# A planned attention and expert kernel: the first three pairs' operands prepared another way, EPS moved into the sums' tiles, and the order planned again

## The chip, the cores and the metric

The kernel runs on one core of one Trainium2 chip. The metric is device microseconds of one execution. The engines are called PE (TensorE, matmul), DVE (VectorE), ACT (ScalarE), POOL (GpSimd) and SP (SyncE, which here issues most of the transfers; POOL issues the rest).

## What is computed

Windowed attention with a linear position bias over 8 batches of 8 heads (S = 576, D = 64), whose output x (8 x 576 x 512) goes into a layer of four attention experts, of which each position takes the two that its gate ranks highest:

```python
scores = scale * q @ k.T                       # per batch and head, 576 x 576
scores = where((rel >= 0) & (rel < 128), scores + slope[h] * -abs(rel), -1e9)
attn = exp(scores - max);  attn /= attn.sum(-1) + 1e-9
x = (attn @ v) with the heads side by side     # B, 576, 512
w = softmax over the top 2 of x @ w_gate       # of 4 experts
for e in range(4):
    a = exp(causal(scale * (x @ wq[e]) @ (x @ wk[e]).T) - max);  a /= a.sum(-1) + 1e-9
    out += w[e] * (a @ (x @ wv[e]) @ wo[e])
```

All of it is float32, and the matmuls run on pairs of rounded operands: a high part and the low rest.

## The kernel before

The heads are taken two at a time: 32 pairs, g = 0 to 31, four to a batch. A pair's raw q and k come in as one tile `r` (128 partitions: one head's 64 dimensions on the upper half and the other's on the lower; q in columns 0 to 575, k in the rest). From it the kernel wants `h`, which holds the rounded high part of q and of k in a layout of its own, the low rest of q written into the other half of the same tile (`h<-r,h` in the rows), and the low rest of k in `klA` (`klA<-r,h`). Two subtractions on half of the partitions each make the one, and two the other; they run on DVE for the pairs 0 and 3 and on POOL else.

Before the change the high part of pair 0 comes by two transfers that POOL issues (`in_hd` holds the same numbers already laid out, and the transfer rounds them), that of pair 1 is rounded on the chip by eight copies from `r` (`rnd`, L428: on POOL or ACT), and from pair 2 on it comes by one POOL transfer a pair (`load_hi`, L499). There are two `h` buffers and one raw buffer `r`; pair 1's `r` lies in a buffer of the tag `v2`, which the expert part uses later (`load`, L480).

Then a pair goes through: scores `s` on PE from h and klA; mask (`COPY_PREDICATED` with `mkt`) and bias with the row's minimum into `nm` on DVE, `p` by an exponential on ACT (`p<-p,nm`) that also leaves the row's sum in `sm`; `normalise` (L606) on DVE adds EPS to the sums (`r<-sm`) and takes the reciprocal, and nine scalings of p by it (`p<-p,r`, `scl`, L434: POOL or ACT, each 128x128) follow; transposes `t` on PE, `pa` on DVE or ACT, the output `x` on PE, and its high and low part `xh` on ACT and DVE. When a batch's four pairs are through, the expert part projects `xh` with the weights WH and WL (made at the start from four staged loads `wst`), and again makes scores `ms`, exponentials `mp`, sums `msm`, `moe_norm` (L856: `mr<-msm`, then scalings on POOL), transposes, values and the output rows `ot`. KHm, QSm, QZm, AHm, AHTm are high parts of its operands, rounded copies that may lie on more than one engine. The attention of the next batch runs beside the experts of the last.

The order is not the order in the text. Every operation is recorded, those that `nc.any` names with several engines, and `plan` (L364) builds the dependence graph and runs a list scheduler (`schedule`, L248) over it: each operation has a rank by its distance to the end plus an offset by the kind of tile it writes (`K['off']`, one number for a kind and an engine), an operation with a choice goes to the engine on which it would be done first by the planner's costs (`_cost`, L57), weighted and biased by `wt`, `bv`, `ba` and `bp`, and a result that crosses engines is charged a latency that `K['lm']` lengthens. Where PE has nothing to do before a set time, the planner puts in a filler, a 128x256 matmul on the zeroed tile QZm that is never read (`warm`, L542; its name in the rows is `warm<-QZm`). All engines then run the planned order, fixed at build time. Since every operation is issued from one place, all rows of the trace name line L1130.

```python
rnd(qs[0][d, :S], r[dn, :S])      # load_hi, d = up, dn: 64x576, two of the eight roundings of pair 1
rnd(kh[0][d], r[up, S:])
```

Of the kernel before, what the change touches and what calls it, by code (L numbers as in the profile page):

```python
# [10 lines left out]
F32 = mybir.dt.float32  # L11
F32R = mybir.dt.float32r
# [22 lines left out]
K = {'sub': '01101', 'S': 2, 'T': 2, 'A': 2, 'X': 1, 'M': 1, 'apv': 0, 'alag': 2, 'pvlag': 2, 'vorder': 0, 'na': 0, 'pp': 2, 'tp': 4, 'mp': 4, 'ta0': 0.08, 'ta1': 0.91, 'sa0': 0.1, 'sa1': 1.0, 'sb0': 0.68, 'sb1': 0.77, 'tb0': -0.03, 'tb1': 1.08, 'wo0': 0.1, 'wo1': 0.45, 'wa0': 0.05, 'wa1': 1.3, 'aa0': 0.0, 'aa1': 1.04, 'ab0': -0.04, 'ab1': 1.0, 'xp': 5, 'sp': 'h||q0 k0|q1|k1', 'ts': 1, 'lead': 0, 'pa': 1, 'na0': 2, 'wb0': 0.18, 'wb1': 1.0, 'sh': 0, 'man': 1, 'mode': 'rank', 'wv': 1, 'off': {'AHms': -17666, 'QSmv': -252, 'outs': -101984, 'KHmg': -413974, 'mps': -362123, 'mrv': -147, 'mptls': -12718, 'hv': 201556, 'mst': 544, 'klv': -1407, 'mpv': -164993, 'wsts': -39692, 'idts': 30423, 'mslt': -3598, 'pv': 145397, 'ots': -67973, 'wv': 612, 'QSms': 238851, 'malt': 978, 'mpts': 16944, 'mtlt': 925, 'pg': -121184, 'mat': -557, 'QDmg': 12259, 'QDmv': 8479, 'AHTms': 59664, 'rv': 59092, 'xtt': 172643, 'vv': 20187, 'vts': -31342, 'rs': 41611, 'cntv': 129924, 'mtt': 1799, 'MPLv': -1030, 'ALTmv': -3669, 'exv': -3931, 'WLv': -330, 'pas': -78677, 'mtts': -135375, 'klg': -78, 'MPLg': -2850, 'tbts': -14292, 'mpg': 26252, 'QZmv': -10712, 'ps': 33824, 'tmts': -456520, 'tms': -205980, 'ALmv': -22397, 'WOHg': -11820, 'WOLv': 42451, 'vs': 5270, 'Qv': 221304, 'KLmg': 67871, 'exs': -162797, 'vg': 16350, 'wsv': 1100, 'wg': -45799, 'MPLs': -10841, 'klAv': 118649, 'xhs': 143747, 'vt': 847, 'mkts': -1800, 'exg': 12657, 'Gg': -11111, 'mxv': -5689, 'KLmv': -28553, 'sv': 8239, 'xhv': 131107, 'klAg': 17772, 'WHg': -29134, 'hg': 26552, 'pav': 144, 'ot': -5058, 'qkt': -18, 'KHms': -16548, 'tt': 859, 'st': 2712}, 'cw': 6, 'lm': 85, 'f0': 900, 'f1': 69640, 'f2': 6176, 'e0': 0, 'setup': 7620, 'wt': 1.0164, 'bv': 4000, 'ba': 634, 'bp': 3635, 'chn': 150, 'e1': 1, 'wu': 0, 'r1': 1, 'l0': 0.5, 'l1': 0.75, 'w0': 0.04, 'w1': 0.83, 'w2': 0.15, 'w3': 1.15}  # L35
# [21 lines left out]
def _cost(e, m, a, k):  # L57
# [20 lines left out]
    return (260 if isinstance(a[2], float) else 244) + 0.84 * n  # L78


def _half(a):
    if a[0].ap[0][1] != D:
        return 0
    return 1 if a[0].offset // a[0].ap[0][0] < D else 2
# [74 lines left out]
def graph(ops, alt):  # L159
# [49 lines left out]
    return dict(port=port, half=half, cat=cat, nodes=nodes, two=two, pred=pred, eng=eng, cost=cost, alts=alts, cols=cols, dma=dma, kind=kind, lab=lab)  # L209
# [38 lines left out]
def schedule(g, rank, succ, setup=0.0, wt=0.5, bias=(0, 0, 0, 0, 0), fill=(900, 60000, 9999), cw=6):  # L248
# [22 lines left out]
    while done < n:  # L271
        while ev and ev[0][0] <= now:
            i = heapq.heappop(ev)[1]
            q = alts[i]
            if len(q) > 1:
                r = rank[i]
                best = None
                for x, (e, c) in enumerate(q):
                    f = max(t[e], now) + c + wt * c + bias[e]
                    for z, j in ready[e]:  # L280
                        if -z > r:
                            f += cost[j]
                    if best is None or f < best[0]:
                        best = (f, e, c, x)
# [5 lines left out]
        for e in range(5):  # L290
            if not ready[e] or t[e] > now:
                continue
            if e == 0 and setup and len(ready[0]) > 1:
# [4 lines left out]
                i = best[1]  # L298
            else:
# [11 lines left out]
            elif e < 4:  # L311
                if half[i] and last[e] and half[i] != last[e]:
                    s = max(s, t[e] + 125)
# [904 lines left out]
```

## Time and profile before

| | us |
|---|---|
| median of 3 runs | 604.6 (603.01 to 606.43) |
| the profiled execution, its own time | 604.72 |
| its span, first to last instruction | 603.0 |
| PE busy | 579.4 (96%), 4697 matmuls |
| ACT busy | 509.5 (84%) |
| DVE busy | 425.9 (71%) |
| POOL busy | 301.1 (50%) |

Busy time counts instructions that overlap once. In rows of a group, the busy time divided by the count is what one instruction takes of its engine; the mean in ns that stands beside it contains the overlap with the next. The granted clock of PE is given as a share of 2.4 GHz: 1.00 is that level and 0.50 is 1.2 GHz.

### The profile page before, as it was taken

Reading aid. Unit: us, or ns where it says so; the run is one execution under the profiler, and the core shown is the slowest. Engines: PE = TensorE matmul, PEld = TensorE weight load, DVE = VectorE, ACT = ScalarE, POOL = GpSimd, SP = SyncE. Lnnn points to the kernel's source line nnn. Section 1 sums busy time; section 2 is a strip of 40 time slices with the busy share of each in tenths; the row PEclk is TensorE's granted clock in tenths of the full one; section 3 lists DMA queues with packets and bytes.
Section 4 is the critical chain, followed back from the end, with each engine's and each line's share of the span. In section 5 each row is a group of like instructions: output and inputs, shape, how many; then the busy total and the mean of one; then the engine's idle time right before and its main releaser. Section 6 shows DMA issues by size and latency. Waiting matters only on the chain.

```text
span 603.0 us, 14062 instructions
## 1 busy us (share of the span) xinstructions
PE 579.4 (96%) x4697; PEld 493.6 (82%) x4697; DVE 425.9 (71%) x1768; ACT 509.5 (84%) x1745; POOL 301.1 (50%) x366
## 2 busy tenths in 40 slices
PE   7999999999999999999999999999999999999996
PEld 7978898788878897888878897888987888789764
DVE  3699869867886689666985689756896669544730
ACT  1987979998989889988999988898999888775973
POOL 3826645676466445473656445674455632023430
PEclk8999999999999999999999999999999999999999
DMA  8496745423544444524345335434444400110013
GB/s 310 133 322 209 248 134 196 146 68 118 168 133 165 146 146 145 198 76 143 107 169 190 123 108 175 154 108 146 143 147 178 155 27 23 54 36 2 1 53 106
DMA packets 24857, 81.50 MB, mean 135 GB/s; under 512 B 2385, under 2 KB 3153, under 8 KB 24785
## 3 DMA queue, kind: packets, MB, share of 16 engines
q1 hardware_dynamic: 16336, 42.00, 21.1%
q0 software_dynamic: 8448, 38.60, 19.0%
q8 instruction: 37, 0.61, 0.4%
q14 instruction: 36, 0.29, 0.2%
HBM read 71.16 MB, written 9.44 MB: 134 GB/s over the span
## 4 chain that ended last, share of the span: by engine, by line
PE 47%; ACT 27%; DVE 15%; DMA 4%; issue 4%; POOL 2%; ACTq 0%; POOLq 0%; DVEq 0%
ACT p L1130 11%; PE qk L1130 8%; PE v L1130 8%; PE s L1130 5%; PE o L1130 5%; PE mt L1130 5%; PE ms L1130 4%; DVE pa L1130 3%; PE t L1130 3%; ACT KHm L1130 3%; ACT mp L1130 3%; PE ma L1130 3%; PE x L1130 2%; DVE r L1130 2%; DVE p L1130 2%
## 5 line engine op out<-in xcount | busy, mean ns | idle before, releaser
L1130 ACT ACTIVATE p<-p,nm 128x128 f32<-128x128 f32 x288 | 113.2, 396 | 29.2 <-DVE nm L1130 28.2
L1130 POOL TENSOR_TENSOR h<-r,h 64x576 fp32r<-64x576 f32 x60 | 85.2, 1420 | 90.5 <-DMA h<-in_hd 55.7
L1130 PE MATMUL qk<-xh,WH 128*128 128x288 f32 x512 | 115.8, 306 | 1.1 <-ACT xh L1130 0.8
L1130 POOL TENSOR_SCALAR mp<-mp,mr,w 128x128 f32<-128x128 f32 (+3 forms) x128 | 76.0, 606 | 64.9 <-DVE mr L1130 57.5
L1130 ACT ACTIVATE p<-p,r 128x128 f32<-128x128 f32 x288 | 98.7, 398 | 9.7 <-DVE r L1130 8.4
L1130 PE MATMUL s<-h 128*128 128x256 f32 (+2 forms) x320 | 87.0, 296 | 3.1 <-DVE h L1130 1.8
L1130 PEld LDWEIGHTS qk<-xh,WH 128*128 128x128 f32 x512 | 84.4, 189 | 4.2 <-ACT xh L1130 1.1
L1130 POOL TENSOR_TENSOR klA<-r,h 64x576 fp32r<-64x576 f32 x60 | 85.2, 1420 | 2.4
L1130 PE MATMUL s<-klA,h 128*128 128x256 f32 (+2 forms) x320 | 84.1, 281 | 0.2 <-POOL klA L1130 0.2
L1130 DVE TENSOR_TENSOR pa<-t,tmt 128x512 f32<-128x512 f32 (+2 forms) x96 | 73.9, 772 | 10.0 <-PE t L1130 6.1
L1130 DVE CUSTOM_DVE_ANT_0 p<-s,tbt 128x128 f32<-128x128 f32 x288 | 72.4, 286 | 3.3 <-PE t L1130 0.6
L1130 ACT ACTIVATE mp<-mp,mnm 128x256 f32<-128x256 f32 (+3 forms) x128 | 71.5, 562 | 3.8 <-DVE mnm L1130 3.5
L1130 DVE COPY_PREDICATED s<-mkt,s 128x256 f32<-128x256 int32 (+2 forms) x160 | 52.6, 331 | 29.9 <-PE s L1130 28.9
L1130 PEld LDWEIGHTS s<-h 128*128 128x128 f32 x320 | 60.5, 190 | 15.3 <-issue 7.2
L1130 PE MATMUL qk<-xh,WL 128*128 128x288 f32 x256 | 71.0, 302 | 0.0
L1130 DVE CUSTOM_DVE_ANT_0 mp<-ms,mtt 128x128 f32<-128x128 f32 (+3 forms) x128 | 59.7, 486 | 15.1 <-PE ms L1130 13.5
L1130 PE MATMUL v<-WH,xh 128*128 128x260 f32 x288 | 65.8, 297 | 0.2 <-DVE lg L1130 0.2
L1130 PE MATMUL x<-pa,vt 128*64 128x256 f32 (+1 forms) x512 | 62.7, 359 | 0.5 <-DVE pa L1130 0.5
L1130 PEld LDWEIGHTS s<-klA,h 128*128 128x128 f32 x320 | 60.6, 192 | 1.2 <-issue 0.6
L1130 PE MATMUL mt<-idt,mp 128*128 128x128 f32 x320 | 59.3, 277 | 1.8 <-DVE ALTm L1130 0.4
L1130 PE MATMUL t<-idt,p 128*128 128x128 f32 x288 | 52.5, 277 | 7.2 <-ACT AHm L1130 2.0
L1130 ACT ACTIVATION_READ_ACCUMULATOR p<-p,nm 128x1 f32 x288 | 54.8, 190 | 0.0
(112 smaller groups left out, 1389.5 us busy)
## 6 DMA issues: line engine op xcount, KB each, us to landing
h<-in_hd POOLq DMA_DIRECT2D x30, 1216.0 KB, 6.4
r<-in_rd SPq DMA_DIRECT2D x31, 576.0 KB, 3.9
vt<-in_vd SPq DMA_DIRECT2D x32, 320.0 KB, 3.1
out<-ot SPq DMA_DIRECT2D x32, 256.0 KB, 2.0
wst<-in_wall SPq DMA_DIRECT2D x4, 386.0 KB, 4.8
h<-in_hd POOLq DMA_DIRECT2D x2, 608.0 KB, 7.7
out<-ot SPq DMA_DIRECT2D x8, 128.0 KB, 2.3
r<-in_rd SPq DMA_DIRECT2D x2, 288.0 KB, 3.0
```

What stands on the lines that cost most here:

```text
L1130: getattr(getattr(tc.nc, e), m)(*a, **k)
```

## The change

**The beginning.** Pair 0's high part is now rounded on the chip, by eight copies that may also go to DVE (`rnd3`), and pair 1's comes by a POOL transfer. Pair 2's goes by two POOL transfers into two of the four expert buffers `mp` that are not yet in use, and pair 2's raw tile into a third. The raw tile of pair 1 and its values come ahead of most tables on SP's queue, the output weights and later tables behind pair 2's raw tile.

**EPS.** The sums get a place of their own with EPS as a neighbouring element, set once at the start (`SM`, `MSM`). A reduction over each sum and its neighbour takes the place of the addition of a constant: 64 `r<-sm` and 48 `mr<-msm` on DVE. Eight small copies `lg<-lg` become additions from PSUM.

**The planner.** Its rule for engines that switch between upper and lower partitions looks at the output and the first input, operations on ACT, DVE and POOL are chosen so that such switches are fewer (`hs`), offsets and biases are given apart for four phases of the program (the beginning, batch 0, the middle, the last batch), `lm` falls from 85 to 15, and all offsets are new. As built, 106 of the 288 scalings `p<-p,r` move from ACT to POOL (3 to 5 of the nine of a pair, from pair 5 on), with them 23 of 64 second roundings of KHm (`KHm<-KHm`) and 14 of 32 `QZm<-QSm`; 9 of 16 `AHTm`, 5 of 16 `AHm` and 4 of 32 `xh<-xt` move from ACT to DVE. There are 181 fillers in place of 209.

```diff
-K = {'sub': '01101', ... 'off': {...}, 'lm': 85, ... 'setup': 7620, 'wt': 1.0164, 'bv': 4000, 'ba': 634, 'bp': 3635, ...}
+K = {'wd': 0, 'sub': '01101', ... 'off': {...}, 'lm': 15, ... 'setup': 8000, 'wt': 0.6887, 'bv': 322, 'ba': -520, 'bp': -651, ...
+     'hs': 5017, 'h4': 'cdmd', 'ra': 'rvm', 'bz': [10885, -12379, 30216]}
 def _half(a):
-    if a[0].ap[0][1] != D:
-        return 0
-    return 1 if a[0].offset // a[0].ap[0][0] < D else 2
+    x = [q for q in a[:2] if _is_ap(q)]
+    return sum((q.offset // q.ap[0][0] >= D) << i for i, q in enumerate(x))
 def schedule(...):
+            elif 0 < e < 4 and hs and len(ready[e]) > 1:
+                best = min(heapq.nsmallest(cw, ready[e]), key=lambda q: q[0] + (hs if half[q[1]] != last[e] else 0))
...
+    def rnd3(dst, src):
+        nc.any(
+            ("gpsimd", "tensor_scalar", (dst, src, 1.0, 0.0), dict(op0=mul, op1=add)),
+            ("scalar", "copy", (dst, src), None),
+            ("vector", "tensor_copy", (dst, src), None),
+        )
+    SM = [cp.tile([P, 9, 2], F32, name=f"sm{k}") for k in range(2)]
+    MSM = [cp.tile([P, 19], F32, name=f"msm{k}") for k in range(2)]
 def load(g):
+        home = K["ra"][g] if g < len(K["ra"]) else "r"
-        if g == 1 and K["r1"]:
+        if home == "v":
             r = m1.tile([P, NQ + 1, E * D], F32, tag="v2", ...)
+        elif home == "m":
+            r = m1.tile([P, 10 * P], F32, tag="mp", name=f"r{g}", bufs=K["mp"])[:, : 2 * S]
 def load_hi(g):
+        how = K["h4"][g] if g < len(K["h4"]) else "d"
+        if how == "m":
+            hh = [m1.tile([P, 10 * P], F32R, tag="mp", name=f"h{g}_{k}", bufs=K["mp"])[:, :o1] for k in range(2)]
...
-        if (g or K["e0"]) and g <= K["e1"]:
+        if how == "c":
             for d in (up, dn):
-                rnd(qs[0][d, :S], r[dn, :S])
-                rnd(kh[0][d], r[up, S:])
+                rnd3(qs[0][d, :S], r[dn, :S])
+                rnd3(kh[0][d], r[up, S:])
...
+        elif how == "m":
+            for k in range(2):
+                o = (o1 + P) * k
+                nc.gpsimd.dma_start(hh[k], hd[b, p, :, o : o + o1])
 def normalise(g, c0, c1):
-        nc.vector.tensor_scalar(r[:, c0:c1], sm[:, c0:c1], EPS, None, op0=add)
-        nc.vector.reciprocal(r[:, c0:c1], r[:, c0:c1])
+        nc.vector.tensor_reduce(r, sm[:, c0:c1, :], AX.X, add)
+        nc.vector.reciprocal(r, r)
 def moe_norm(b, pr, j):
-            nc.vector.tensor_scalar(r, sm[:, 4 * j : 4 * j + 4], EPS, None, op0=add)
+            nc.vector.tensor_reduce(r, sm[:, 8 * j : 8 * j + 8].rearrange("p (a n) -> p a n", n=2), AX.X, add)
 def zero():
+            nc.vector.memset(SM[k][:, :, 1], EPS)
+            nc.vector.memset(MSM[k][:, 1:16:2], EPS)
+            nc.vector.memset(MSM[k][:, 18:19], EPS)
 # the beginning of the program
+    load(1)
+    nc.sync.dma_start(loaded_vt[0], vd[0, 0])
     load_const_b()
     prep0()
-    load(1)
```

Three places of the planned order show it. First PE at the start, before the change; `warm2` is the filler, s0_0 to s0_4 are the five score tiles of pair 0:

```order
L1130 MATMUL warm2_112<-QZm_99 128x256 x26
L1130 MATMUL s0_0_118<-h0_110 128x128
L1130 MATMUL warm2_112<-QZm_99 128x256 x3
L1130 MATMUL s0_1_120<-h0_110 128x256
L1130 MATMUL warm2_112<-QZm_99 128x256 x6
L1130 MATMUL s0_0_118<-klA0_96,h0_110 128x128
```

and now:

```order
L1163 MATMUL warm2_116<-QZm_103 128x256 x37
L1163 MATMUL s0_0_121<-h0_114 128x128
L1163 MATMUL s0_0_121<-klA0_100,h0_114 128x128
L1163 MATMUL s0_0_121<-h0_114 128x256
L1163 MATMUL s0_0_121<-klA0_100,h0_114 128x256
L1163 MATMUL s0_1_123<-h0_114 128x256
```

The first block of fillers has grown from 26 to 37, and the scores of pair 0 follow in one piece.

Second, ACT at the start, before the change; h1 and r1 belong to pair 1, p0 and p1 to the pairs 0 and 1, WOH is the high part of the output weights:

```order
L1130 ACT_TABLE_LOAD
L1130 ACTIVATE p0_117,sm0_116<-p0_117,nm0_115 128x128 x4
L1130 CAST WOH_94<-wst4_162 128x1024
L1130 ACTIVATE p0_117,sm0_116<-p0_117,nm0_115 128x128 x3
L1130 CAST h1_119<-r1_113 64x576 x2
L1130 ACTIVATE p0_117,sm0_116<-p0_117,nm0_115 128x128 x2
L1130 CAST h1_119<-r1_113 64x576 x5
L1130 ACTIVATE p0_117<-p0_117,r0_0_122 128x128
```

and now:

```order
L1163 ACT_TABLE_LOAD
L1163 CAST h0_114<-r0_112 64x576 x8
L1163 ACTIVATE p0_120,sm0_96<-p0_120,nm0_119 128x128 x6
L1163 ACTIVATE p0_120<-p0_120,r0_0_125 128x128 x5
L1163 ACTIVATE p0_120,sm0_96<-p0_120,nm0_119 128x128 x3
L1163 ACTIVATE p0_120<-p0_120,r0_5_128 128x128 x4
```

The seven roundings of pair 1 are gone from between the exponentials of pair 0, and eight roundings of pair 0 stand ahead of them.

Third, POOL some pairs in, before the change; h6, h7 and klA belong to the pairs 6 and 7:

```order
L1130 TENSOR_TENSOR h6_217<-r6_211,h6_217 64x576 x2
L1130 TENSOR_TENSOR klA0_96<-r6_211,h6_217 64x576 x2
L1130 TENSOR_TENSOR h7_239<-r7_233,h7_239 64x576 x2
L1130 TENSOR_TENSOR klA1_97<-r7_233,h7_239 64x576
L1130 DMA h8_261<-in_hd 128x2x1216
L1130 TENSOR_TENSOR klA1_97<-r7_233,h7_239 64x576
```

and now:

```order
L1163 TENSOR_TENSOR h6_216<-r6_211,h6_216 64x576 x2
L1163 DMA h7_237<-in_hd 128x2x1216
L1163 TENSOR_TENSOR klA0_100<-r6_211,h6_216 64x576 x2
L1163 TENSOR_SCALAR p5_214<-p5_214,r5_5_229 128x128 x2
L1163 TENSOR_SCALAR KHm_106<-KHm_106 64x288
L1163 TENSOR_TENSOR h7_237<-r7_232,h7_237 64x576 x2
L1163 TENSOR_TENSOR klA1_101<-r7_232,h7_237 64x576
L1163 DMA h8_258<-in_hd 128x2x1216
L1163 TENSOR_TENSOR klA1_101<-r7_232,h7_237 64x576
L1163 TENSOR_SCALAR p6_235<-p6_235,r6_5_250 128x128 x2
```

Scalings of p (of pairs 5 and 6) and a rounding of KHm now stand in POOL's queue behind the subtractions that need a transferred h, and ahead of the next ones.

## Rows read from the trace of the kernel before

**Rows 1.** The page, part 1 (busy time, share of the span and instructions of each engine) and part 4 (the chain that ended last, by engine).
```profile
PE 579.4 (96%) x4697; PEld 493.6 (82%) x4697; DVE 425.9 (71%) x1768; ACT 509.5 (84%) x1745; POOL 301.1 (50%) x366
...
PE 47%; ACT 27%; DVE 15%; DMA 4%; issue 4%; POOL 2%; ACTq 0%; POOLq 0%; DVEq 0%
```

**Rows 2.** Busy time in four stretches: the stretch and its length, then PE, PE's weight loads, DVE, ACT and POOL with their instructions, the granted clock, the DMA share and GB/s.
```profile
0.00:75.00 75.00, 70.19 (x547) 61.45 (x548) 55.75 (x208) 54.91 (x198) 41.35 (x44) 0.98 0.73 244
75.00:525.00 450.00, 437.48 (x3622) 374.21 (x3621) 338.35 (x1430) 400.64 (x1403) 238.56 (x285) 1.00 0.40 133
525.00:560.00 35.00, 34.93 (x264) 30.10 (x262) 17.30 (x74) 25.07 (x72) 9.18 (x19) 1.00 0.08 24
580.00:604.00 24.00, 17.51 (x129) 12.51 (x127) 2.45 (x8) 10.33 (x23) 2.27 (x4) 0.94 0.28 100
```

**Rows 3.** The timeline of PE at the start (start, duration, engine, line, operation, tiles, and the idle time before with what ended it), and the fillers as a whole (count, duration min/median/max in ns, first and last start).
```profile
1.53 5.88 PE L1130 MATMUL warm<-QZm 128*128 128x256 f32 x26 [1.53 <-DVE QZm L1130]
9.19 0.33 PE L1130 MATMUL s<-h 128*128 128x128 f32 x1 [1.78 <-DVE h L1130]
...
16.71 4.36 PE L1130 MATMUL warm<-QZm 128*128 128x256 f32 x35
...
L1130 PE MATMUL warm<-QZm x209: 274/283/581, 1.5 to 68.7; 128*128 128x256 f32 x105
```

**Rows 4.** Two stretches at the start, columns as in group 2.
```profile
7.40:9.20 1.80, 0.02 (x2) 0.01 (x1) 0.48 (x2) 0.00 (x0) 0.00 (x0) 1.00 1.04 355
10.60:14.00 3.40, 3.40 (x19) 3.40 (x18) 2.87 (x11) 0.41 (x3) 0.00 (x0) 0.51 1.04 403
```

**Rows 5.** Transfers, the page's part 6: count, KB each, median us from issue to landing.
```profile
h<-in_hd POOLq DMA_DIRECT2D x30, 1216.0 KB, 6.4
...
h<-in_hd POOLq DMA_DIRECT2D x2, 608.0 KB, 7.7
...
r<-in_rd SPq DMA_DIRECT2D x2, 288.0 KB, 3.0
```

**Rows 6.** The timeline of ACT at the start, and one row of POOL's, columns as in group 3.
```profile
13.59 0.40 ACT L1130 ACTIVATE p<-p,nm 128x128 f32<-128x128 f32 x1 [11.58 <-DVE nm L1130]
...
17.37 1.37 ACT L1130 CAST h<-r 64x576 fp32r<-64x576 f32 x2
...
19.55 3.44 ACT L1130 CAST h<-r 64x576 fp32r<-64x576 f32 x5
...
23.61 0.39 ACT L1130 ACTIVATE p<-p,nm 128x128 f32<-128x128 f32 x1
...
0.73 1.05 POOL L1130 MEMSET KLm<- 64x1152 f32 x1 [0.29 <-POOLq L1203]
```

**Rows 7.** Groups of instructions on ACT: count, busy us, mean ns of one, idle time before them and what ended it.
```profile
L1130 ACT ACTIVATE p<-p,r 128x128 f32<-128x128 f32 x288 | 98.7, 398 | 9.7 <-DVE r L1130 8.4 <-DVE lg L1130 0.5
L1130 ACT CAST KHm<-KHm 64x288 fp32r<-64x288 f32 x64 | 26.9, 430 | 1.0
L1130 ACT CAST AHm<-ma 128x512 fp32r<-128x512 f32 x16 | 9.2, 576 | 0.6 <-PE ma L1130 0.5
L1130 ACT CAST QZm<-QSm 128x64 fp32r<-128x64 f32 x32 | 7.5, 242 | 1.2 <-DVE QSm L1130 0.5
L1130 ACT CAST h<-r 64x576 fp32r<-64x576 f32 x7 | 4.7, 672 | 0.2
```

**Rows 8.** Groups of instructions on POOL, columns as in group 7.
```profile
L1130 POOL TENSOR_TENSOR h<-r,h 64x576 fp32r<-64x576 f32 x60 | 85.2, 1420 | 90.5 <-DMA h<-in_hd 55.7 <-issue 15.2 <-DMA r<-in_rd 15.2
...
L1130 POOL DMA_DIRECT2D h<-in_hd x32 | 24.1, 753 | 39.2 <-PE s L1130 26.2 <-PE v L1130 10.4 <-PE t L1130 1.5
...
L1130 POOL TENSOR_SCALAR mp<-mp,mr,w 128x128 f32<-128x128 f32 x32 | 14.3, 446 | 64.8 <-DVE mr L1130 57.5 <-ACT AHm L1130 3.4 <-ACT KHm L1130 1.2
```

**Rows 9.** Waits of ACT and of POOL between 75 and 525 us: who waited for whom, us in total, times, longest.
```profile
ACT p L1130 <- DVE nm L1130: 14.5, 26, 1.3
...
POOL h L1130 <- DMA h<-in_hd: 55.7, 9, 7.9
```

**Rows 10.** The timeline of POOL at 18 and 28 us and of DVE at 30 and 40 us, columns as in group 3.
```profile
18.03 0.66 POOL L1130 TENSOR_SCALAR h<-r 64x576 fp32r<-64x576 f32 x1
...
28.68 2.93 POOL L1130 TENSOR_TENSOR klA<-r,h 64x576 fp32r<-64x576 f32 x2
...
30.34 1.31 DVE L1130 TENSOR_SCALAR r<-sm 128x4 f32<-128x4 f32 x1
...
40.55 0.17 DVE L1130 TENSOR_SCALAR r<-sm 128x4 f32<-128x4 f32 x1
```

**Rows 11.** Groups of instructions on DVE, columns as in group 7.
```profile
L1130 DVE TENSOR_SCALAR r<-sm 128x5 f32<-128x5 f32 x32 | 13.0, 406 | 3.9 <-ACT p L1130 3.8
L1130 DVE TENSOR_SCALAR r<-sm 128x4 f32<-128x4 f32 x32 | 10.2, 320 | 6.8 <-ACT p L1130 6.5
L1130 DVE TENSOR_SCALAR mr<-msm 128x4 f32<-128x4 f32 x32 | 9.0, 282 | 14.8 <-ACT mp L1130 13.0 <-ACT AHTm L1130 1.6 <-POOL mp L1130 0.2
L1130 DVE TENSOR_SCALAR mr<-msm 128x1 f32<-128x1 f32 x16 | 3.4, 210 | 4.4 <-ACT MPL L1130 4.3
L1130 DVE TENSOR_REDUCE ws<-ex 128x5 f32<-128x20 f32 x8 | 1.4, 171 | 0.8 <-POOL ex L1130 0.7
```

**Rows 12.** ACT alone from its first exponential to 75 us: length, busy time and instructions, then clock, DMA share and GB/s.
```profile
13.59:75.00 61.41, 53.63 (x197) 1.00 0.69 231
```

## What is predicted

> **What bounds the kernel now.** I read the page's shares first: PE is busy for 96% of the span and ACT for 84%, and of the chain that ended last 47% is PE and 27% ACT [rows 1]. So PE bounds it, and what can be won is idle time of PE, PE work that does nothing, and PE work at the lower clock. Next I cut the span into stretches [rows 2]. In the steady part, 75 to 525 us, PE is idle for 450.0 - 437.5 = 12.5 us (2.8%) with ACT busy for 400.6 of 450 (89%). From 525 to 560 us, where the last batch's attention is over, ACT is at 25.1 of 35 (72%) and PE idle for 0.07 us (0.2%). That pair of rows makes ACT a suspect for PE's gaps, not more: DVE and POOL have less to do there too.
>
> The third view is the timeline of PE at the start [rows 3]. Most of it is filler: 26 of them from 1.53 us, then nothing to 9.19 us, where the first score of pair 0 starts, and 35 between 16.71 and 21.1 us, where PE has done pair 0's scores and waits for pair 1's. The fillers count as busy, so the 94% of the first 75 us [rows 2] is not work. The fourth view is the granted clock in small stretches [rows 4]: 1.00 from 7.40 to 9.20 us, 0.51 from 10.6 to 14.0. The lower level is 1.2 GHz; what lies ahead of it is that 1.8 us, in which PE ran almost nothing (0.02 us). The end, 580 to 604 us [rows 2], has the same output rows behind it in both orders, and I expect nothing there.
>
> **The beginning.** Before, pair 0 waits for its h, which two transfers on POOL's queue bring 7.7 us after their issue, while its raw tile lands after 3.0 us [rows 5]. ACT does nothing of weight until its first exponential at 13.59 us [rows 6]. Now eight roundings from the raw tile make h on ACT in that free time. The raw tile is the first transfer on SP's queue, issued when the engines start at 0.7 us [rows 6], so they start at about 0.7 + 3.0 = 3.7 us; one takes 4.7 / 7 = 0.67 us of ACT [rows 7], the first seven end at about 3.7 + 7 x 0.67 = 8.4 us, and the fillers planned ahead last to 7.41 + 11 x 4.36 / 35 = 8.8 us [rows 3]. So the roundings are covered by fillers, and the cover is 0.4 us; if the raw tile lands later than that, PE stands still again. Three terms follow:
> - 28 fillers fewer (209 to 181) at 4.36 / 35 = 0.125 us [rows 3]: -3.4 us. A filler is only padding, so this is real only as far as the waits it covered are shorter too; the next paragraph checks that on ACT.
> - The hole of 1.8 us between 7.40 and 9.20 [rows 4] is closed: -1.8 us.
> - Without the hole I expect no fall of the clock: 3.4 us ran at half the clock [rows 4], and the same work at 2.4 GHz takes half: -1.7 us.
>
> Together -6.9 us. The check by ACT: the first exponential can come at about 10.1 us instead of 13.59, because the seventh rounding ends at 8.4 and the scores, the mask and the bias need the rest (-3.5), and the seven roundings of pair 1 that stood among pair 0's exponentials, 1.37 + 3.44 us [rows 6], leave ACT's queue (-4.7). So ACT allows at most 8.2 us. The lower bound is 0: the time could be lost again at the next wait. What is late next is pair 1. Its h now comes by one transfer of 1216 KB; issued at about 3.1 us, behind two POOL memsets of 1.05 us that begin at 0.73 [rows 6] and two small ones, it lands at 9.5 us by the median of 6.4 [rows 5], up to 1.3 later by the 7.7 us that the first two took while the tables loaded. Behind it four POOL subtractions of 1.42 us and 0.75 us of the issue of pair 3's transfer [rows 8] end at 16 to 17.3 us. By then ACT has nine exponentials and nine scalings of pair 0 to do from 10.1 us on, which end near 17 us. So the new wait is about covered, and I take the 6.9, which lies near the upper bound because three rows carry it one by one.
>
> **The steady part.** What leaves ACT, each by busy time over count [rows 7]: 106 scalings of p at 0.343 (36.3 us), 23 KHm at 0.420 (9.7), 14 QZm at 0.234 (3.3), 5 AHm at 0.576 (2.9), and 9 AHTm and 4 xh of the same 128x64 as the QZm at up to 0.234 (3.0): 55.2 us, of which I put nine tenths, some 49 us, into 75 to 525 us. ACT falls to (400.6 - 49) / 450 = 78%. On a straight line between 89% (PE idle 2.8%) and 72% (0.2%) that is 1.1%, a gain of 7.5 us. Since the quiet stretch is quiet on other engines too, I take half of PE's idle time, -6.2 us. The bounds are 0 (PE's gaps have other causes: of ACT's own waits the largest is for `nm` from DVE, 14.5 us [rows 9], which a lighter ACT doesn't shorten) and the whole 12.5.
>
> What POOL takes on: 106 x 0.446 (a scaling of this size there, [rows 8]) = 47.3 us, and 37 casts: a 64x288 lies between that and the 0.66 us of a 64x576 ([rows 10]), a 128x64 below it, some 17 us, together 64 us. POOL goes from 301 to 365 us, 61% of the span; it has no bound of its own there. It has long waits for a transferred h, 55.7 us [rows 9], and the scalings now stand behind them: that is the slower rival.
>
> **EPS as an element.** 112 additions on DVE, 13.0 + 10.2 + 9.0 + 3.4 = 35.6 us, become reductions; the nearest row, a reduction of more elements, takes 0.171 us [rows 11], so 112 x 0.171 = 19.2 us, 16.4 us less on DVE. The reason to believe it is one place: an addition of 128x4 that takes 0.17 us alone took 1.31 us and ended at 31.65, when a pair of POOL's subtractions ended at 31.61 [rows 10]; the addition was held. If the reductions are held alike, the gain is 0. DVE is at 71% and this is at most 0.14 us an instruction on the way to the scalings, so I add nothing for it; it is one reason why half of PE's idle time and not less goes away, and if it fails I take half of that, -3.1.
>
> The Trainium skill (SBUF — State Buffer, section Who interferes with whom) says that DVE and GpSimd have one pair of ports in common under an exclusive lock, that a DVE addition of this kind may take it and that on trn2 a reduction never does. The row of the addition agrees (1.31 us against 0.17); for a reduction beside POOL's work no row here shows it. By the rule the 16.4 us are sure and the sum is as below; without it the steady term is halved, 594.7.
>
> **The sum**, against the profiled execution's own 604.7 us, 0.1 above the median: 604.7 - 3.4 - 1.8 - 1.7 - 6.2 +- 0 at the end = **591.6 us**.
>
> **Rivals.** A measurement of this kernel tells about 0.5%, 3.0 us, from no change.
> - *Forecast case*: 591.6, own range 585 to 597, chance 0.46.
> - *The beginning alone*: PE's steady gaps are not ACT's, 604.7 - 6.9 = 597.8. For it speaks that ACT waits for `nm`; against it the pair of stretches. 0.17.
> - *The steady part alone*: pair 1's subtractions on POOL end after 17.3 us and become a wait that eats the beginning, 604.7 - 6.2 = 598.5. 0.09.
> - *Lock*: POOL's 64 us of new work hold DVE where it still adds, copies or takes two inputs. Now 35.6 - 112 x 0.17 = 16.6 us of DVE are held under 301 us of POOL [rows 1, 11]; at that rate 64 us hold 3.5 us more, and all on the path gives 591.6 + 3.5 = 595.1. 0.06. By the rule cited above this holds only for DVE work with two inputs on chip, or for its copies and additions.
> - *No net effect*: 28 fillers become plain idle time, since a wait has the length that its data set, and the new order has its own gaps: 601.6 to 607.6. 0.12.
> - *Slower*: POOL's queue becomes the wait. The scalings of pair g stand behind the subtractions of pair g+1 on POOL, and these wait for a transferred h (55.7 us now, [rows 9]), which no p waited for; the transposes on PE wait for p. If a quarter of that reaches PE, 13.9 us, the steady gain is gone, and the beginning stands, the sum is 604.7 - 6.9 + 13.9 = 611.7. It decides from the point where an eighth of the waits reaches PE (6.9 us, 0.26 us for each of the 27 pairs concerned). Against it: the planner may place 3 to 5 scalings of nine on POOL and keeps ACT for the others, and POOL's share stays at 61%. 0.10.
>
> **How the numbers follow.** Faster by over 0.5%: 0.46 + 0.17 + 0.09 + 0.06 = 0.78; within: 0.12; slower: 0.10. The range goes from 604.7 - 8.2 (all of ACT's room at the start) - 3.9 (half of ACT's idle 7.8 us from 13.59 to 75 us, [rows 12]) - 12.5 = 580 us up to 603, which takes in all cases on the faster side and the lower edge of no net effect; left out are the slower case and most of no net effect, 0.2.
>
> **What would show it.** In the profile after: the first score of pair 0 at 8.8 to 9.2 us straight behind the fillers, the granted clock at 1.00 from 9 to 16 us, and the first exponentials of the pairs 0 and 1 at about 10 and 17 to 18 us (now 13.6 and 23.6). Then ACT at 75 to 80% of the stretch between the same places of the program, PE idle there for about 6 us, `r<-sm` and `mr<-msm` near 0.17 us each. It would be wrong if PE waits there for p from POOL, if POOL's waits for h grow, or if pair 1's scores wait for klA beyond 18 us.

## The result, and the profile after

The changed kernel takes 583.7 us (median of 4 runs, 581.48 to 584.53) beside 603.8 us for the kernel before on the same chip: a ratio of 0.9647, 95% interval 0.9619 to 0.9674, 20 us less. The forecast was 591.6 in a range of 580 to 603. The profiled execution took 584.46 us, its span 582.7. First the page of the changed kernel, parts 1 and 4, beside [rows 1]:

```profile
PE 568.9 (98%) x4669; PEld 491.4 (84%) x4669; DVE 414.9 (71%) x1793; ACT 467.1 (80%) x1585; POOL 349.0 (60%) x507
...
PE 68%; DVE 16%; ACT 11%; issue 2%; DMA 1%; POOL 1%; ACTq 0%; DVEq 0%; POOLq 0%
```

ACT is down from 84% to 80% of a shorter span, POOL up from 50% to 60%, and the chain that ended last is now two thirds PE, with ACT at 11% instead of 27%. To see where the 20 us went, the program has to be cut at the same places. With PE's real work as the ruler, what had been done at 75.59 us before is done at 71.00 us after, and what had been done at 544.89 us at 525.00 us. The two stretches (kernel before, then after; columns as in [rows 2]) hold 3757 and 3758 matmuls:

```profile
75.59:544.89 469.30, 456.77 (x3757) 391.22 (x3757) 346.46 (x1463) 415.36 (x1443) 243.67 (x293) 1.00 0.39 129
```
```profile
71.00:525.00 454.00, 450.48 (x3758) 391.59 (x3757) 340.22 (x1482) 374.83 (x1288) 292.83 (x432) 1.00 0.40 134
```

So the beginning gave 4.6 us and the steady part 469.3 - 454.0 = 15.3 us; the rest, the end, is 58.1 us before and 57.7 after. The steady part can be relied on: five of the kernels below that differ from the changed one only in the beginning take 453.8 to 454.0 us for it. The beginning varies from one execution to the next: in three kernels below that begin in the order of before it lasts 74.8 to 75.4 us (75.59 here), in two that begin in the order of the changed kernel 71.68 and 67.84 (71.00 here), so its gain lies between 3 and 8 us. In the steady part PE's idle time fell from 12.5 to 3.5 us. The other 6.3 us are in its busy time, 456.8 to 450.5 us for the same matmuls: the profile models their ends, so a wait between two pipelined matmuls can lie in it. ACT is busy 374.8 / 454.0 = 83% (88.5% before).

The beginning, PE's timeline after (columns as in [rows 3]) and two stretches of it (as in [rows 4]):

```profile
1.45 7.19 PE L1163 MATMUL warm<-QZm 128*128 128x256 f32 x37 [1.45 <-DVE QZm L1163]
8.49 0.29 PE L1163 MATMUL s<-h 128*128 128x128 f32 x1
...
12.37 1.83 PE L1163 MATMUL warm<-QZm 128*128 128x256 f32 x14
17.08 0.30 PE L1163 MATMUL t<-idt,p 128*128 128x128 f32 x1 [2.89 <-ACT p L1163]
...
17.86 3.59 PE L1163 MATMUL warm<-QZm 128*128 128x256 f32 x17
```
```profile
14.20:17.10 2.90, 0.02 (x1) 0.05 (x1) 0.34 (x2) 2.40 (x11) 2.76 (x4) 1.00 1.07 407
18.00:20.40 2.40, 2.40 (x13) 2.40 (x13) 0.00 (x0) 0.00 (x0) 2.33 (x3) 0.50 1.05 420
```

The hole of [rows 4] is closed: pair 0's scores follow the fillers at 8.49 us. But a new one of 2.9 us stands before the first transpose at 17.08 us, and behind it the clock falls to 0.50, so 17 fillers take 3.59 us. That fall is not in every execution: of the four, two have a mean granted clock of 0.995 and 0.996 and take 584.5 us each, and two have 0.999 and 1.000 and take 581.5 and 583.0. The trace names ACT's p as what ended the wait, but the scalings of p concerned had ended by 14.6 us; what came last is the identity matrix for the transpose, by the transfers (columns as in [rows 5]) and the rows of POOL and ACT:

```profile
h<-in_hd POOLq DMA_DIRECT2D x3, 1216.0 KB, 10.0
...
idt<-in_ident SPq DMA_DIRECT2D x1, 64.0 KB, 12.5
```
```profile
3.01 2.02 POOL L1163 DMA_DIRECT2D h<-in_hd  x3
...
13.08 2.88 POOL L1163 TENSOR_TENSOR h<-r,h 64x576 fp32r<-64x576 f32 x2 [5.80 <-DMA h<-in_hd]
...
16.73 2.88 POOL L1163 TENSOR_TENSOR klA<-r,h 64x576 fp32r<-64x576 f32 x2
```
```profile
9.87 0.40 ACT L1163 ACTIVATE p<-p,nm 128x128 f32<-128x128 f32 x1 [0.91 <-DVE nm L1163]
...
22.79 0.41 ACT L1163 ACTIVATE p<-p,nm 128x128 f32<-128x128 f32 x1
```

The identity is 64 KB, was issued at 4.5 us and landed 12.5 us later, at 17.0. In two of the kernels below (the additions put back, the scalings put back on ACT), which begin in the same order, it landed 11.7 and 10.4 us after its issue, and the first transpose started at 16.45 and 15.05 us; in the first of them the trace names it:

```profile
16.45 0.30 PE L1168 MATMUL t<-idt,p 128*128 128x128 f32 x1 [2.37 <-DMA idt<-in_ident]
```

So it is the identity that the transpose waits for. Pair 1's h took 10.0 us and not 6.4, so POOL's subtractions ran from 13.08 to 19.6 us instead of ending by 17.3, and pair 1's first exponential came at 22.79 us. From 5 to 24 us the transfers move about 390 GB/s, and in the two stretches above the share of the 16 DMA engines is 1.07 and 1.05.

Last the groups that answer to [rows 7, 8, 11]:

```profile
L1163 ACT ACTIVATE p<-p,r 128x128 f32<-128x128 f32 x182 | 61.2, 394 | 9.6 <-DVE r L1163 8.1 <-DVE cnt L1163 1.0
L1163 POOL TENSOR_SCALAR p<-p,r 128x128 f32<-128x128 f32 x106 | 37.8, 368 | 42.1 <-DVE r L1163 34.6 <-DVE mr L1163 2.2 <-ACT xh L1163 2.1
...
L1163 DVE TENSOR_REDUCE r<-sm 128x4 f32<-128x8 f32 x32 | 5.1, 160 | 12.8 <-ACT p L1163 12.3
L1163 DVE TENSOR_REDUCE mr<-msm 128x4 f32<-128x8 f32 x32 | 5.0, 157 | 3.1 <-ACT mp L1163 1.3 <-ACT xh L1163 0.9 <-ACT AHTm L1163 0.5
L1163 DVE TENSOR_REDUCE r<-sm 128x5 f32<-128x10 f32 x32 | 5.0, 155 | 4.5 <-ACT p L1163 4.3
L1163 DVE TENSOR_REDUCE mr<-msm 128x1 f32<-128x3 f32 x16 | 2.4, 150 | 5.3 <-ACT MPL L1163 4.2 <-POOL mp L1163 1.0
```

The 112 reductions take 17.5 us together where the additions took 35.6, and none takes over 0.17 us. By busy time over count a scaling of p takes POOL 0.36 us and ACT 0.34.

### The profile page after: what moved, and what is told of

It is laid out like the page before. It is cut to its first block, busy times and chain, and to the rows that moved or that the text cites. A ratio compares the mean times of both kernels' runs of the same rounds, so it can differ in the third digit from the quotient of the medians.

```text
span 582.7 us, 14070 instructions
## 1 busy us (share of the span) xinstructions
PE 568.9 (98%) x4669; PEld 491.4 (84%) x4669; DVE 414.9 (71%) x1793; ACT 467.1 (80%) x1585; POOL 349.0 (60%) x507
## 4 chain that ended last, share of the span: by engine, by line
PE 68%; DVE 16%; ACT 11%; issue 2%; DMA 1%; POOL 1%; ACTq 0%; DVEq 0%; POOLq 0%
PE qk L1163 12%; PE v L1163 9%; PE o L1163 8%; PE s L1163 8%; ACT p L1163 5%; PE mt L1163 5%; PE ms L1163 5%; PE x L1163 4%; PE ma L1163 4%; PE t L1163 4%; DVE pa L1163 4%; PE warm L1163 3%; PE msl L1163 2%; DVE p L1163 2%; DVE s L1163 2%
## 5 line engine op out<-in xcount | busy, mean ns | idle before, releaser
L1163 PE MATMUL qk<-xh,WH 128*128 128x288 f32 x512 | 117.6, 310 | 1.5 <-ACT xh L1163 0.6
L1163 PEld LDWEIGHTS qk<-xh,WH 128*128 128x128 f32 x512 | 82.7, 189 | 5.1 <-ACT xh L1163 2.1
L1163 PE MATMUL s<-h 128*128 128x128 f32 (+2 forms) x320 | 84.4, 290 | 0.0
L1163 ACT ACTIVATE mp<-mp,mnm 128x384 f32<-128x384 f32 (+3 forms) x128 | 71.7, 562 | 11.4 <-DVE mnm L1163 10.3
L1163 DVE CUSTOM_DVE_ANT_0 mp<-ms,mtt 128x512 f32<-128x512 f32 (+3 forms) x128 | 59.1, 486 | 26.0 <-PE ms L1163 25.3
L1163 ACT ACTIVATE p<-p,r 128x128 f32<-128x128 f32 x182 | 61.2, 394 | 9.6 <-DVE r L1163 8.1
L1163 DVE COPY_PREDICATED s<-mkt,s 128x128 f32<-128x128 int32 (+2 forms) x160 | 51.8, 331 | 21.3 <-PE s L1163 19.9
L1163 POOL TENSOR_SCALAR p<-p,r 128x128 f32<-128x128 f32 x106 | 37.8, 368 | 42.1 <-DVE r L1163 34.6
L1163 PE MATMUL v<-WH,xh 128*128 128x260 f32 x288 | 60.5, 294 | 0.0
L1163 PE MATMUL t<-idt,p 128*128 128x128 f32 x288 | 56.6, 277 | 3.4 <-ACT p L1163 2.9
```

Of the source, the lines that this page charges most:

```text
L1163: getattr(getattr(tc.nc, e), m)(*a, **k)
```

## The experiments

Each of the swaps below keeps the planned order: the plan is made as in the kernel named, and then single instructions are replaced in the finished list, so that nothing else moves. Ratios are to the kernel before in the same runs. Since PE runs the same matmuls in the same order in a kernel and its swap, each matmul's start can also be set beside that of its twin; the differences, summed by what the matmul makes, say where PE gains time in the steady part. Two kernels that differ only in the beginning agree there to 0.4 us for each kind.

**The additions of EPS put back into the changed kernel.**

```diff
 nc.vector.tensor_reduce(r, sm[:, c0:c1, :], AX.X, add)
+swap[...] = ("vector", "tensor_scalar", (r, sm[:, c0:c1, 0], EPS, None), dict(op0=add))   # at emission; moe_norm alike
```

> The changed kernel in its planned order; only the 112 reductions over sum and EPS are additions of a constant again, as before. Load theory (the steady gain is ACT's lighter queue): the additions take 0.3 to 0.4 us where POOL is at work, up to 16 us more on DVE, little of it on the path: 584 to 588 us, ratio to before 0.966 to 0.973. Lock theory (the steady gain comes from reductions that are not held): most of the 15 us is lost, 592 to 597 us, ratio 0.980 to 0.988. Order theory (the gain belongs to the new order as a whole): as the load theory, 583 to 586.

592.4 us, ratio 0.9791 (0.9768 to 0.9815): 8.7 us of the 20 are lost by 112 small instructions on DVE. The additions are held again (the two groups of the run):

```profile
L1168 DVE TENSOR_SCALAR r<-sm 128x5 f32<-128x5 f32 x32 | 12.0, 374 | 4.8 <-ACT p L1168 4.6
L1168 DVE TENSOR_SCALAR r<-sm 128x4 f32<-128x4 f32 x32 | 10.5, 328 | 12.3 <-ACT p L1168 11.8
```

Of the 112, 33 take over 0.25 us; 28 of these end within 0.08 us of the end of one of POOL's subtractions or scalings, and 4 more with the end of POOL's issue of a transfer. Of the other 79, 21 end near the end of a POOL instruction. The steady part is 6.0 us longer:

```profile
71.68:531.69 460.01, 451.99 (x3758) 391.94 (x3757) 354.02 (x1482) 375.57 (x1288) 293.87 (x433) 1.00 0.39 131
```

By the twins PE loses 2.7 us of it at the output rows `o` (they need AHm), 1.8 at the projections `qk` (they need xh) and 1.1 at the scores `s`. The tiles are those of the changed kernel, so the instruction alone makes this difference. The median lies at the lower edge of what the lock theory expected and 4 us beyond the load theory's upper edge.

**Reductions in the kernel before.** The same swap the other way. It brings the tiles of the change along: the sums with the stored EPS and six memsets for it, `r` with five columns, and `ws` in the buffer of `mx`.

```diff
+swap[...] = ("vector", "tensor_reduce", (r, sm[:, c0:c1, :], AX.X, add), {})
```

> The kernel before in its planned order; only the 112 additions of EPS are reductions over sum and a stored EPS, with the six memsets for it. Load theory: 600 to 604 us, ratio 0.995 to 1.000. Lock theory: 590 to 597 us, ratio 0.978 to 0.988. Order theory: 0.997 to 1.000.

598.5 us, ratio 0.9892 (0.9874 to 0.9910), 6.5 us faster: by the ratio 0.001 short of what the lock theory expected and 0.006 beyond the load theory. DVE's busy time falls by 15.3 us (425.9 to 410.6), PE's idle time between the two places from 12.5 to 9.5 us. Of ACT's waits between 75 and 525 us, the one for r falls from 4.3 to 2.3 us and the one for `nm` from 14.5 to 13.1. The steady part is 5.5 us shorter:

```profile
75.39:539.16 463.77, 454.25 (x3757) 391.11 (x3757) 334.87 (x1462) 414.55 (x1442) 244.50 (x294) 1.00 0.39 131
```

By the twins 2.2 us of that are gained at the outputs `x` and `xt`, which need `pa`, 1.2 at the expert scores `ms`, which need QSm, and 0.9 at the scores `s`, but only 0.3 at the transposes of p. So the gain comes less through the scalings, for which the sums are needed, than through other work of DVE, which issues in order and has the additions in its queue. Three of the 112 reductions take 0.28 us here; each stands behind an instruction `cnt<-cnt` that ended with POOL's issue of a transfer.

**The scalings of p put back on ACT in the changed kernel.**

```diff
+if e == "gpsimd" and m == "tensor_scalar" and re.match(r"p\d+_|p\d+$", a[0].tensor.name):
+    e, m, a, k = "scalar", "mul", a[:3], {}
```

> The changed kernel in its planned order; only the 106 scalings of p on POOL run on ACT, at the same place of the order. Load theory: ACT gains 36 us and PE waits for p and for ACT's copies again, 590 to 597 us, ratio 0.977 to 0.988. Lock theory: POOL is freed of 38 us, so nothing is lost, 580 to 585. Order theory: the order was planned for the other engine, so 585 to 590.

605.7 us, ratio 1.0002 (0.9981 to 1.0023): the whole gain is gone, which none of the three theories expected. In a profiled execution of 601.6 us the same places of the program are 474.3 us apart (454.0), and PE's idle time there is 18.3 us. Of its waits between 75 and 525 us the two longest, 12.4 us together, are for ACT's xh and mptl, which the plan had put behind an emptier queue. By the twins PE loses 9.7 us at the transposes `t` of p and 6.5 us at `qk`.

```profile
67.84:542.18 474.34, 456.06 (x3757) 391.26 (x3757) 339.13 (x1482) 404.00 (x1394) 256.90 (x328) 1.00 0.38 128
```
```profile
PE qk L1165 <- ACT xh L1165: 6.8, 5, 1.4
PE t L1165 <- ACT mptl L1165: 5.6, 5, 1.1
```

**The same scalings moved to POOL in the kernel before.**

```diff
+if t and e == "scalar" and m == "mul" and str(a[0].offset % 1152 // 128) in POOLP.get(int(t.group(1)), ""):
+    e, m, a, k = "gpsimd", "tensor_scalar", a + (0.0,), dict(op0=mul, op1=add)
```

> The kernel before in its planned order; only the same 106 scalings (same pair, same block) run on POOL instead of ACT, at the same place of the order. Load theory: 592 to 598 us, ratio 0.980 to 0.990, PE idle between 75 and 525 us falls from 12.5 to about 6 us. Lock theory: POOL holds DVE's additions longer, 603 to 608. Order theory: the order does not suit it, 600 to 608.

597.2 us, ratio 0.9863 (0.9840 to 0.9885), as the load theory had it, in an order that was not planned for it. PE's idle time between 75 and 525 us fell less than expected, from 12.5 to 9.2 us; the steady part is 5.5 us shorter all the same. By the twins PE gains 6.1 us at the transposes `t` of p and 1.6 at those of the experts, `mt`, and loses 2.2 elsewhere. The waits of `t` for ACT, 3.9 us in the kernel before, fall to 0.7 (for mptl), those for DVE from 2.8 to 1.3. The three before:

```profile
PE t L1130 <- ACT AHm L1130: 2.0, 3, 0.7
...
PE t L1130 <- ACT AHTm L1130: 1.0, 1, 1.0
PE t L1130 <- ACT p L1130: 0.9, 1, 0.9
```

So ACT was most of what these transposes waited for. With the reductions alone the same three waits for ACT stay at 2.0, 1.0 and 0.9 us. (By the list in the edit 2 to 6 of a pair's nine scalings move, not 3 to 5.) Two things beside it: POOL's waits for a transferred h fell from 55.7 to 22.3 us, where the scalings now stand, and the additions `r<-sm` of five columns were held longer than before:

```profile
74.83:538.66 463.83, 454.65 (x3757) 391.85 (x3757) 349.61 (x1461) 388.68 (x1337) 282.38 (x399) 1.00 0.39 131
```
```profile
POOL h L1134 <- DMA h<-in_hd: 22.3, 5, 5.9
```
```profile
L1134 DVE TENSOR_SCALAR r<-sm 128x5 f32<-128x5 f32 x32 | 15.4, 480 | 3.3 <-ACT p L1134 3.2
```

0.48 us instead of 0.41 [rows 11], and all 112 additions take 39.1 us instead of 35.6: in this order POOL's new work costs DVE time as long as the additions are there. It is not so in every order: with the additions put back into the changed kernel (above) the 112 take 35.2 us beside 350 us of POOL's work, no more than before beside 301.

**Both in the kernel before**, by the two edits above.

> The kernel before in its planned order with both edits that paid singly: reductions for the EPS additions (0.989 alone) and 106 scalings of p on POOL (0.986 alone). If the two gains add up: 0.976, 590 to 592 us, and nothing of the steady gain is left to the new order itself. If both relieve the same wait: 0.983 to 0.987, 595 to 597. If the reductions matter more with POOL busier, since additions were then held longer (0.48 against 0.41 us): 0.970 to 0.974, 586 to 589.

591.6 us, ratio 0.9775 (0.9721 to 0.9829). The interval is too wide to tell the sum from a little more. By the trace it is a little more: between the two places of the program the kernel before takes 469.3 us, with the reductions 463.8, with the scalings on POOL 463.8, with both 456.3, that is 5.5 and 5.5 alone and 13.0 together. The changed kernel takes 454.0, so taken last, the other 55 moved casts and the new order are worth 2.3 us.

```profile
75.24:531.52 456.28, 450.63 (x3757) 391.75 (x3757) 334.09 (x1461) 387.55 (x1337) 281.79 (x399) 1.00 0.40 133
```

**Program and planner apart.** The new program planned with the old numbers and rules (`parts_old_plan`), and the old program with the new ones.

```diff
-K = {... new offsets, 'lm': 15, 'hs': 5017, ...}
+K = {... offsets of before, 'lm': 85, 'hs': 0, 'h4': 'cdmd', 'ra': 'rvm', ...}     # and the old _half
```

> The program of the change (beginning, EPS as an element) planned with the numbers and rules of the planner of before. If the parts add up: the reductions give 6 us and the beginning 4, 593 to 596 us, ratio 0.980 to 0.985. If the new numbers are needed for the beginning to pay: 598 to 601, 0.989 to 0.994. If the old numbers do not suit the new program at all: 603 or more.

> The program of before (transfers for pair 0, EPS added as a constant) planned with the numbers and rules of the new planner. If the parts add up: the scalings on POOL and the order give 8 us, 595 to 598 us, ratio 0.984 to 0.990. If the new order gives more than the scalings: 588 to 593, 0.972 to 0.981. If the numbers suit only the new program: 600 or more.

599.8 us, ratio 0.9912 (0.9886 to 0.9939), and 610.4 us, ratio 1.0075 (1.0049 to 1.0101). The sums expected of the parts came out in neither. The first reaches the place of 71.00 us at 70.3, so the beginning pays under the old numbers too, but its steady part takes 468.6 us although it has the reductions, which gave 5.5 us where the order was kept. The second needs 82.4 us for the beginning and 468.7 us for the steady part. Numbers that were found for one program give away several us on another, more than a part of this change is worth; why in single places was not pursued.

**Pair 0's h by transfers again, in the changed kernel.**

```diff
-8 x scalar.copy(h0 <- r0), 2 x gpsimd.memset(h0)
+gpsimd.dma_start(h[:, :o1], hd[0, 0, :, :o1]); gpsimd.dma_start(h[:, o1:], hd[0, 0, :, o1 + P :])
```

> The changed kernel in its planned order; only pair 0's rounded part comes by two transfers on POOL's queue, as before, ahead of those of the pairs 1 and 2, and the eight roundings on ACT are gone. If the rounding on chip is what shortens the beginning: 4 to 8 us more, 587 to 591 us, ratio 0.971 to 0.978, first score of pair 0 at 10 us or later. If pair 1's operands set the beginning anyway: 583 to 586, 0.964 to 0.969.

591.9 us, ratio 0.9768 (0.9721 to 0.9814): 8 us more, though the steady part is the same 453.9 us. Pair 0's h now shares the transfers with those of the pairs 1 and 2 and lands at 13.6 us; PE starts 6.5 us later. So this prices the transfer beside those of the new beginning, not the beginning of before, where no other pair's h was under way and the first score started at 9.19 us [rows 3]:

```profile
14.98 0.47 PE L1174 MATMUL s<-h 128*128 128x128 f32 x1 [6.53 <-DVE h L1174]
```

**Waits of the beginning taken out one by one**, in the changed kernel: the identity ahead of pair 1's raw tile on SP's queue; pair 1's four subtractions on DVE (those of q right ahead of those of k); both; both, with 712 KB of tables and pair 3's transfer moved back.

```diff
+seq_.insert(i, seq_.pop(j))     # idt's load ahead of r1's
+if e == "gpsimd" and m == "tensor_tensor" and ...: e = "vector"     # h1, klA1 from r1
```

> The changed kernel in its planned order; only the load of the identity matrix stands ahead of pair 1's raw tile on SP's queue instead of behind the values. If PE's 2.9 us before the first transpose are a wait for the identity (it lands at about 17.0 us, the scalings of p end at 14.6): the first transpose at 14.3 us, no fall of the clock behind it, 1 to 2 us gained, 581 to 583 us, ratio 0.961 to 0.966. If it is a wait for p or for a free PSUM buffer: the first transpose at 17 us as before and 583 to 585.

> The changed kernel; only the four subtractions of pair 1 (low part of q, then of k) run on DVE, which is idle from 13.8 to 22 us, instead of POOL. They end at about 17 us instead of 19.6. If pair 1's klA sets the next stage: its scores 2 us earlier, 581 to 583 us, 0.961 to 0.965. If the transfers of pair 2 set it: the same 583 to 585.

> Both edits of the beginning: identity loaded early, pair 1's subtractions on DVE. If each removes a wait of its own: 2 to 4 us, 579.5 to 582 us, ratio 0.959 to 0.962. If the transfers are the bound of the beginning (about 400 GB/s from 5 to 24 us): at most 1 us, 582 to 584.

> The changed kernel with the identity loaded early and pair 1's subtractions on DVE, and now also what is needed late moved behind what is needed first: the output weights and the mask table (712 KB) behind pair 3's raw tile, their rounding ahead of the first rounding of WH, pair 3's transfer (1216 KB) behind pair 2's subtractions of q. If the transfers set the beginning, pair 2's raw tile lands some 4 us sooner than the 18.7 to 23.3 us of the other variants, PE reaches the same place 2 to 4 us earlier, 579 to 582 us, ratio 0.957 to 0.962. If pair 2 is held by something else, or the late loads are missed later: 583 to 588, 0.964 to 0.972.

Ratios 0.9626 (0.9592 to 0.9660), 0.9657 (0.9628 to 0.9685), 0.9682 (0.9646 to 0.9718) and 0.9679 (0.9652 to 0.9706): none differs from the changed kernel's 0.9647 beyond the intervals. In order they are 582.2, 584.4, 586.4 and 585.5 us. The identity did land early and the first transpose started at 14.02 us; the next wait then stood at pair 1's h, and the clock fell behind that one:

```profile
14.02 0.27 PE L1166 MATMUL t<-idt,p 128*128 128x128 f32 x1
16.73 0.50 PE L1166 MATMUL s<-h 128*128 128x128 f32 x2 [2.44 <-POOL h L1166]
```
```profile
18.00:20.00 2.00, 2.00 (x13) 2.00 (x12) 0.00 (x0) 0.00 (x0) 1.93 (x2) 0.55 1.04 420
```

With pair 1 on DVE alone its subtractions ended at 19.87 us, not at 17, since DVE waited 2.8 us for PE's scores between the first and the second. On POOL the wait moved on to pair 2's raw tile, for which POOL waited 5.6 us, to 19.45 us, with both edits 9.6 us, to 23.28 us in a profiled execution of 590.2 us. With the late loads moved back POOL's first subtraction of pair 2 still started only at 19.04 us, against the expectation of 4 us sooner, and DVE stood still for 3.4 us, to 28.63 us, ahead of pair 3's subtractions: the transfer that the edit had moved back landed at 28.55. What follows stands in all of them, shown for the last and for the changed kernel: pair 4's raw tile goes into the one raw buffer, its transfer is issued when DVE's subtractions of pair 3 have ended (32.75 us in the changed kernel, 31.69 here), and POOL waits for it to 36.77 and 36.13 us:

```profile
19.04 2.90 POOL L1188 TENSOR_TENSOR h<-r,h 64x576 fp32r<-64x576 f32 x2 [11.76 <-DMA r<-in_rd]
...
36.13 2.90 POOL L1188 TENSOR_TENSOR h<-r,h 64x576 fp32r<-64x576 f32 x2 [9.81 <-DMA r<-in_rd]
```
```profile
36.77 2.89 POOL L1163 TENSOR_TENSOR h<-r,h 64x576 fp32r<-64x576 f32 x2 [7.57 <-DMA r<-in_rd]
```

So each wait that was removed gave way to the landing of the next operand, and pair 2's start, 0.5 us earlier with all edits (19.04 us against 19.58), was worth 0.6 us at pair 4's raw tile. That another order of the loads brings time was not confirmed; a second raw buffer, which the traces point to, was not tried.

## Why the prediction was right or wrong

*Direction and mechanism* held: ACT's queue and the beginning were where time could be won. The gain was half as large again as forecast, 20 us against 13.1. It lies below the forecast's own 585 to 597 us and inside the outer range, and that by some luck: the steady part gave 15.3 us, more than the 12.5 of PE's idle time that the prediction took as its most, and the beginning less than its most. The bound failed because 6.3 us of the gain lie in PE's busy time.

*EPS, predicted 0*: this is the step that failed. The prediction counted 16.4 us less on DVE, put them off the path because DVE was at 71% and an instruction lost little, and used them only as a condition of the steady term. The swaps gave 6.5 us alone (5.5 in the steady part) and 8.7 us undone (6.0). Its 0.14 us an instruction, called the most, is the mean (16.4 / 112 = 0.15): its own row has one that lost 1.14 us. DVE runs its instructions in order here, so what is held with an addition is all that stands behind it (the `pa` behind the addition of [rows 10] started at 31.56 us), and the twins show PE's gain there, at `x`, `xt`, `ms` and `s` before and at `o`, `qk` and `s` after. A share of busy time does not show that. The price of one reduction was right (0.171 us predicted, 0.150 to 0.160 measured), and so was the row it rested on: of the 36 additions that took over 0.25 us in the kernel before, 30 end with one of POOL's subtractions or scalings and 4 with its issue of a transfer. The Trainium skill (SBUF — State Buffer, section Who interferes with whom) says that on trn2 a reduction never contends with GpSimd. The trace agrees: in the changed kernel none of the 112 takes over 0.17 us beside 349 us of POOL's work.

*The scalings, predicted -6.2 as half of PE's idle time*: 5.5 us alone in the trace, 8 us by the runs, the right size, and by the path that was named: PE gained at the transposes of p, whose waits for ACT went. The size is in part luck, since PE's idle time fell by 3.3 us only, from 12.5 to 9.2. ACT fell by 40.5 us between the two places of the changed kernel, not by 49. The rows of the moved work did fall by the 55 us that were counted, but rows of different groups overlap: all of ACT's groups add up to 624 us before where ACT is busy for 509.5. So a row's busy time over its count is more than its removal frees, and ACT is at 83% and not 78%.

*What was left out* is that the two work on each other: 11.0 us apart, 13.0 together. A likely part of the reason is that POOL's new work held the additions longer in that order, by 3.5 us in all; more is not shown. The prediction had that as the lock rival's price, 3.5 us for 64 us of new work on POOL, and as a loss only. The new order itself, taken last, gave 2.3 us.

*The beginning, predicted -6.9* (its first term is 28 x 4.36 / 35 = 3.5 and not 3.4): 4.6 us measured. The fillers fell to 181, the first hole closed, the first exponential came at 9.87 us (10.1 predicted). The term of the clock, -1.7, failed in the profiled execution: the clock was at 1.00 from 9 to 14 us and at 0.50 behind the new hole. What stood in place of the predicted cover is the landing of pair 1's h, 10.0 us after its issue where 6.4 to 7.7 were taken from transfers of a quieter time, and that of the identity, which the prediction did not look at. In the kernel with the scalings put back on ACT, which begins in the same order, the identity landed about 2 us earlier, PE waited 0.8 us, the clock stayed at 1.00, and the place of 75.59 us was reached at 67.84, 7.8 us sooner. The prediction said that pair 1 is what is late next; it priced that too low, and one of its signs of being wrong came true: pair 1's scores with klA started at 21.42 us, beyond 18.

*Rivals*: the lock rival had the mechanism of the held additions, with the sign the other way. The slower case asked whether POOL's waits for h would reach PE; between 75 and 525 us they fell from 55.7 to 7.6 us, with scalings and casts placed into them. POOL rose to 349 us and not 365, since a scaling took it 0.36 us and not the 0.446 of the row that was used. The reverse of that fear showed: with the scalings left on ACT in the new order the whole gain is lost.

## What to carry to other kernels

On an engine that issues in order, price a held instruction by what stands behind it and who waits for that, not by the engine's share of busy time or the mean of its group; the idle time of the busiest engine in a profile is not a sure upper bound of what can be won; a small instruction on every chain is worth an experiment of its own. Test the parts of a replanned kernel with the order kept: planned anew, the steady part of the program with reductions came out 5 us longer than with the order kept. At the start of a kernel, take the landing time of a transfer from the bytes that are under way with it, and go through every operand of the first instruction of each kind, the small tables too.

## What the runs showed of the hardware

A DVE addition of 128x5 took 0.41 us in the mean beside 301 us of POOL's work and 0.48 us beside 340 us in the same order, and a reduction in its place 0.16 us beside either; in the changed order the addition took 0.37 us beside 350 us. The identity's 64 KB landed 3.3 to 4.7 us after their issue when they were issued ahead of pair 1's raw tile and its h, and 10.4 to 12.5 us behind them. PE's clock fell to 0.50 behind a hole of 2.9 us in the changed kernel, of 2.4 us in the one with the identity loaded early, and to 0.51 behind one of 1.8 us in the kernel before. In the kernel with pair 1's subtractions on DVE it stayed at 1.00 from 10 to 20 us with a hole of 2.4 us at the same place, so the length of the hole alone does not decide:

```profile
10.00:20.00 10.00, 7.34 (x60) 6.82 (x58) 6.35 (x28) 5.99 (x26) 1.25 (x2) 1.00 1.09 401
```
